# Seven block products for eight in 12 of the 16 d_ff tiles of the remaining tokens' second MLP product

## The chip, the cores and the metric

The kernel runs on one core of a Trainium2 chip. The metric is the device time of one execution in microseconds (us). Before the change the median of three runs is 258.58 us (258.47 to 258.95).

The engines are named as in the profile: PE (TensorE, matrix products), PEld (its weight loads), DVE (VectorE), ACT (ScalarE), POOL (GpSimd) and SP (SyncE, which here only issues DMAs).

## The reference

Polynomial-sketch attention, then an MLP with an exact GELU. B = 4 batches, H = 4 heads, S = 1088 tokens, D = 32; d_model = H x D = 128, d_ff = 2048; all in float32.

```python
def phi(x):                      # S1, S2: (8, 32)
    a = np.einsum('rd,bhsd->bhsr', S1, x)
    b = np.einsum('rd,bhsd->bhsr', S2, x)
    return np.einsum('bhsi,bhsj->bhsij', a, b).reshape(*x.shape[:-1], r * r)
q_p, k_p = (phi(q), phi(k))
kv = np.einsum('bhsf,bhsd->bhfd', k_p, v)
z = np.sum(k_p, axis=2)
num = np.einsum('bhsf,bhfd->bhsd', q_p, kv)
den = np.einsum('bhsf,bhf->bhs', q_p, z)[..., None] + 1e-06
x = (num / den).transpose(0, 2, 1, 3).reshape(B * S, H * D)
h = x @ w_in                     # (4352, 128) @ (128, 2048)
g = 0.5 * h * (1.0 + erf(h * inv_sqrt2))
out = g @ w_out                  # (4352, 2048) @ (2048, 128)
```

## The kernel before, in words

**Chunks and tiles.** The 4352 tokens are worked in nine chunks: eight of 512 tokens (n = 0 to 7, two for each batch, the first 1024 tokens of each), and a ninth (n = 8, called NMAIN in the code) of the 256 remaining tokens, 64 of each batch. d_ff is cut into 16 tiles of 128 (fi). A step is one pair (chunk, tile). `hidden` multiplies a tile of w_in by the chunk's transposed x (L739, 512 or 256 moving columns) into a bank of the pool `hps` (two banks), and ACT writes the GELU of it to SBUF (L746), as g in [d_ff, token] form. With `by_halves` the same product is issued as two matmuls of 64 stationary columns each, one for each half of the PE array, which run side by side.

**The second product of chunks 0 to 7.** In most tiles it is done with seven block products in place of eight (the Winograd form of Strassen's algorithm): tokens and channels are cut in halves and two d_ff tiles are the two halves of the inner dimension. POOL makes four sums of the activations (`token_sums`, L790 to L793, for four tiles at a time) and, once, four sums T1 to T4 of the halves of w_out (`channel_sums`, L777 to L780). The products (`two_products`, L825) have 64 stationary columns and run in pairs on the two halves of the PE array; `drain` and `combine` put the results together on DVE and ACT, and `store` transposes and stores them.

**The second product of the ninth chunk.** It is done whole, in [token, channel] form: `project` takes, for each tile, g of 128 tokens as the stationary operand and the tile of w_out (128 x 128) as the moving one, for each of the two token halves (L873; L876 is the same function's matmul for the first tiles of chunks 0 and 1). The two token halves accumulate in two banks, each taken with `work_bank` from the pool `wps`, which has two buffers. `store` copies the first half with DVE and issues its DMA from SP, and copies the second half with ACT and issues its DMA from ACT's queue (L882, L883).

**Order.** The order is written out by hand: for each step t the lists `slots`, `products`, `drains` and `done` say what is issued with it, and at the end every engine's instructions are bound to the order of the text. So PE, POOL, DVE and ACT each work through one fixed queue; an instruction that waits holds up all behind it on its engine. For the ninth chunk, step fi issues the hidden tile fi and then the second products put into that step: the first three tiles' in step 5, two tiles' in step 6, and then tile fi - 2 in step fi. After the last hidden tile, eight products are left, of tiles 12 to 15: three of token half 0, then half 1 of tile 12, the last of half 0, and the other three of half 1.

Of the kernel before, what the change touches and what calls it, by code (L numbers as in the profile page):

```python
# [8 lines left out]
FP = mybir.dt.float32  # L9
# [7 lines left out]
def kernel(  # L17
# [18 lines left out]
    pe, dve, act, pool, sp = nc.tensor, nc.vector, nc.scalar, nc.gpsimd, nc.sync  # L36
# [5 lines left out]
    NF = d_ff // 128  # L42
# [5 lines left out]
    CW = JC * 128  # L48
    G = 128 // 32
    NCH = J // JC  # L50
    C = D + 1
    LAG = 2
    NMAIN = B * NCH
    NB = 4

    USUAL = 8
    NCHUNK = NMAIN + 1
    assert B == 4 and d_model == 128 == H * D == JC * D == 2 * F and H == 4 and REM == 64 and NCH == 2

    big = ctx.enter_context(tc.tile_pool(name="big", bufs=1))  # L60
    att = ctx.enter_context(tc.tile_pool(name="att", bufs=2))
    mlp = ctx.enter_context(tc.tile_pool(name="mlp", bufs=2))
# [8 lines left out]
    def work_bank():  # L71
        return work_banks()[:, 0]
# [11 lines left out]
    by_act, by_dve, by_pool = act.copy, dve.tensor_copy, pool.tensor_copy  # L84
# [12 lines left out]
    w_out_sb = [big.tile([128, c1 - c0], FP, name=f"w_out{i}") for i, (c0, c1) in enumerate(pieces)]  # L97
# [96 lines left out]
    for i, (queue, s) in enumerate(((act, S1), (sp, S2))):  # L194
        s, e = words(s)
# [528 lines left out]
    g_of, o_of = {}, {}  # L724

    def w_tile(w, fi):
        i = max(i for i, (c0, c1) in enumerate(pieces) if c0 <= fi * 128)
        at = fi * 128 - CUTS[i]
        return w[i][:, at:at + 128]
# [3 lines left out]
    def hidden(n, fi, by_halves=False):  # L733
        W = width[n]
        ps = first_banks.pop((n, fi)) if (n, fi) in first_banks else hidden_bank()
        w = w_tile(w_in_sb, fi)
        for rows in (slice(0, 64), slice(64, 128)) if by_halves else (slice(0, 128),):
            if (n, fi) not in begun:
                pe.matmul(ps[rows, :W], lhsT=w[:, rows], rhs=xT[n][:, :W], start=True, stop=True)  # L739
        if n < NCH and fi < USUAL:  # L740
            g_of[n, fi] = mlp.tile([128, CW], FP, name="g", bufs=4)
        else:
            if fi % NB == 0:
                blocks[n, fi // NB] = block(FP)
            g_of[n, fi] = blocks[n, fi // NB][:, fi % NB]
        act.activation(out=g_of[n, fi][:, :W], in_=ps[:, :W], func=ACT.Gelu)  # L746
# [12 lines left out]
    blocks, sums, acc = {}, {}, {}  # L759
    T = {}  # L760
# [67 lines left out]
    drained = {}  # L828
# [26 lines left out]
    def combine(n):  # L855
# [6 lines left out]
            dve.tensor_add(out=N[:, 1], in0=N[:, 1], in1=usual[n])  # L862
        return N[:, 1]

    def project(n, fi, parts=range(B // 2), cols=slice(None)):
        first, final = fi == 0, fi == (USUAL if n < NCH else NF) - 1
        if first:
            o_of[n] = out_bank() if n < NMAIN else [work_bank() for i in range(B // 2)]
        g = g_of[n, fi]
        if n == NMAIN:  # L870

            for i in parts:
                pe.matmul(o_of[n][i][:, :128], lhsT=g[:, i * 128:(i + 1) * 128], rhs=w_tile(w_out_sb, fi),  # L873
                          start=first, stop=final)
            return
        pe.matmul(o_of[n][:, cols], lhsT=w_tile(w_out_sb, fi), rhs=g[:, cols], start=first, stop=final)  # L876

    def store(n):
        oT = mlp.tile([128, JC, d_model], FP, name="oT")
        if n == NMAIN:  # L880
            for i, copy, queue in ((0, by_dve, sp), (1, by_act, act)):
                copy(out=oT[:, i, :], in_=o_of[n][i][:, :128])  # L882
                queue.dma_start(out=out.rearrange("(two b s) d -> two b s d", two=2, s=S)[:, i, MAIN:S, :].rearrange("two s d -> s two d"),  # L883
                             in_=oT[:, i, :])
            return

        dve.transpose(out=oT.rearrange("p n d -> p (n d)"), in_=combine(n))
        row = n // NCH * S + n % NCH * CW
        if n < NCH:

            for c in range(d_model // 32):
                to = out[0:MAIN, c * 32:(c + 1) * 32].rearrange("(g t n j) d -> n j t g d", t=32, n=NCH, j=JC)[n]
                o = oT[c * 32:(c + 1) * 32].rearrange("p n (m d) -> p (n m) d", d=32)
                o = o.rearrange("p (g j) d -> j p g d" if n == 0 else "p (j g) d -> j p g d", j=JC)
                for j in range(JC):
                    sp.dma_start(out=to[j], in_=o[j])
            return
        to = out[row:row + CW].rearrange("(t n) d -> t n d", t=32)
        of = oT.rearrange("p n (m d) -> p (n m) d", d=32)
        for at in (slice(0, 16),) if n != NMAIN - 2 else (slice(0, 8), slice(8, 16)):  # L900
            for c in range(d_model // 32):
                sp.dma_start(out=to[:, at, c * 32:(c + 1) * 32], in_=of[c * 32:(c + 1) * 32, at])
# [46 lines left out]
    for c in range(NP):  # L949
        rows = slice(c * F, (c + 1) * F)  # L950
# [202 lines left out]
    for t, (n, fi) in enumerate(steps):  # L1153
        if n < NCH and fi < USUAL:
            products[t + LAG].append((project, n, fi))
            if fi == USUAL - 1:
                slots[t + LAG + 1 + 2 * n].append(lambda n=n: take_usual(n))
        elif n == NMAIN:
            at_ = max(t + LAG, (n * NF + 5) if fi < 3 else (n * NF + 6) if fi < 5 else 0)
            if fi < NF - 4:  # L1160
                products[at_].append((project, n, fi))
            if fi == NF - 1:

                products[at_] += [(project, n, NF - f, (i,)) for f, i in ((4, 0), (3, 0), (2, 0), (4, 1), (1, 0), (3, 1),
                                                                          (2, 1), (1, 1))]
                done[at_ + 1].append(n)
        elif fi % NB == NB - 1:
            b = fi // NB
            opens = b == first_block(n)
            late = int(n < NCH or n == NCH and opens)  # L1170
            for later, pairs in ((3, 3), (4, 2), (5, 2)) if opens else ((2, 2), (3, 2), (4, 1), (5, 2)):
                later += late
                for i in range(pairs):
                    products[t + later].append((two_products, n, b, len([p for q in products.values() for p in q
                                                                        if p[:3] == (two_products, n, b)])))
            if b == NF // NB - 1:
                drains[t + 6 + late].append(n)
                done[t + 12].append(n)

    for t in range(len(steps) + LAG):  # L1180
        if t < 4:

            hidden(0, t)
            if t == 0:
                expand_multiply(1, 0)
                w_out[0].fields()
                expand_copy(1, 1)
                expand_multiply(1, 1)
            if t == 1:
                w_out[0].low_words()  # L1190
                w_out[0].exponents()
                w_out[0].finish()
                w_out[1].fields()
            if t == 2:
                w_out[1].low_words()
            if t == 3:
                banks = work_banks()
                numerators_by_token(1, halves(banks), range(JC))
                w_out[1].mantissas(by_pool=True)
                w_out[1].exponents()  # L1200
                divide(1, halves(banks), 0)
                w_out[1].signs()
                w_out[1].product()
                project(0, 0)
                project(0, 1, cols=slice(0, 256))
                turn_half(1, 0, work_bank(), by_act)
                project(0, 1, cols=slice(256, 512))
                turn_half(1, 1, work_bank(), by_dve)
            continue
        if t == 4:  # L1210
            first_hidden(1, 0)
            for f, *a in products[t]:
                f(*a)
            first_hidden(1, 1)
        for n in drains[t]:
            drain(n)
        sooner = t == NMAIN * NF
        if sooner:
            for f, *a in products[t]:
                f(*a)  # L1220
        if t < len(steps):
            n, fi = steps[t]
            hidden(n, fi, by_halves=t >= 18 and (n < NMAIN or fi < 5))
        if t < len(steps) and steps[t][0] < NMAIN and steps[t][1] % NB == NB - 1:
            n, b = steps[t][0], steps[t][1] // NB
            if b >= first_block(n):
                token_sums(n, b)
        for f in slots[t]:
            f()
        for n in done[t]:  # L1230
            store(n)
        if t != 4 and not sooner:
            for f, *a in products[t]:
                f(*a)
# [41 lines left out]
```

## Time and profile before

| | |
|---|---|
| median of three runs | 258.58 us |
| the profiled execution's own time | 258.97 us |
| its span, first to last instruction | 257.2 us |
| PE busy | 253.0 us (98%) |
| POOL busy | 164.5 us (64%) |
| DVE busy | 151.6 us (59%) |
| ACT busy | 114.7 us (45%) |
| granted TensorE clock | 1.0 throughout |
| last POOL operation (chunk 7's sums) starts | 238.88 us |
| hidden tile 5 of the ninth chunk starts | 241.85 us |
| ACT's copy of the last output starts | 254.05 us |

How it is read: a PE line counts passes; a float32 matmul is two passes, and the two matmuls that run side by side on halves of the array start within 10 ns of each other. Shapes are written as array rows x stationary columns ("128\*64"), then the moving operand. The duration of one PE instruction contains its way through the array, so the rate is read from the distance between starts.

### The profile page before, as it was taken

To read this page: it belongs to the slowest core of one execution; us is meant where nothing else is said; L and a number is where in the kernel's file an instruction comes from. 1 tells how busy PE (TensorE), PEld (TensorE's weight loads), DVE (VectorE), ACT (ScalarE), POOL (GpSimd) and SP (SyncE) were. 2 spreads that over 40 slices of the span, in tenths; PEclk is the share of its full clock that TensorE was granted. 3 is DMA by queue.
4 is the path that set the end of the run, shared out by engine and by line. 5 is a ranking of instruction groups with operands and counts; after the bars stand their busy time and mean duration, and the time that the engine had idled before them with its cause. 6 is when DMAs were issued, how large, how long until landed. Compare 5 with 4: busy or idle time off the path is not lost.

```text
span 257.2 us, 5633 instructions
## 1 busy us (share of the span) xinstructions
PE 253.0 (98%) x2265; PEld 133.4 (52%) x2265; DVE 151.6 (59%) x314; ACT 114.7 (45%) x222; POOL 164.5 (64%) x175
## 2 busy tenths in 40 slices
PE   8999999999999999999999999999999999999995
PEld 4856444255444545454444455445544444445794
DVE  4896888969698987580278976399307000700330
ACT  3784767533535333533335332623444334433442
POOL 3414007799968787587758774787758777877300
PEclk9999999999999999999999999999999999999999
DMA  6699558710001101102000001000200200020020
GB/s 205 176 320 307 146 128 205 198 17 9 0 0 18 26 4 23 20 10 33 0 3 0 0 15 31 1 4 0 34 10 11 33 0 4 9 32 3 0 41 23
DMA packets 29082, 13.48 MB, mean 52 GB/s; under 512 B 21888, under 2 KB 27264, under 8 KB 29056
## 3 DMA queue, kind: packets, MB, share of 16 engines
q1 hardware_dynamic: 28624, 12.79, 20.2%
q8 instruction: 18, 0.29, 0.5%
q10 hardware_dynamic: 432, 0.33, 0.4%
q14 instruction: 8, 0.07, 0.1%
HBM read 10.88 MB, written 2.23 MB: 51 GB/s over the span
## 4 chain that ended last, share of the span: by engine, by line
PE 98%; ACT 0%; issue 0%
PE h_ps L739 45%; PE o_ps L825 33%; PE o_ps L876 5%; PE w_ps L873 3%; PE w_ps L455 1%; PE w_ps L603 1%; PE w_ps L658 1%; PE w_ps L908 1%; PE w_ps L569 1%; PE h_ps L755 1%; PE h_ps L347 1%; PE o_ps L444 1%; PE w_ps L994 1%; PE w_ps L684 0%; PE o_ps L396 0%; PE w_ps L485 0%
## 5 line engine op out<-in xcount | busy, mean ns | idle before, releaser
L739 PE MATMUL h_ps<-xT,w_in 128*64 128x512 f32 (+3 forms) x514 | 137.0, 576 | 0.0
L746 ACT ACTIVATE block<-h_ps 128x512 f32<-128x512 f32 (+1 forms) x128 | 73.0, 571 | 117.3 <-PE h_ps L739 115.3
L739 PEld LDWEIGHTS h_ps<-xT,w_in 128*64 128x64 f32 (+1 forms) x514 | 41.8, 142 | 30.6 <-issue 11.6
L825 PE MATMUL o_ps<-block,w_out 128*64 128x256 f32 x224 | 57.5, 379 | 0.0
L790 POOL TENSOR_TENSOR bits_low<-block 128x512 f32<-128x512 f32 x28 | 36.1, 1291 | 27.2 <-ACT block L746 27.2
L825 PEld LDWEIGHTS o_ps<-block,w_out 128*64 128x64 f32 x224 | 30.5, 137 | 38.0 <-issue 27.5
L791 POOL TENSOR_TENSOR bits_a<-block 128x512 f32<-128x512 f32 x28 | 35.8, 1277 | 11.7 <-ACT block L746 11.6
L840 DVE COPY sums<-o_ps 64x256 f32<-64x256 f32 x8 | 3.3, 416 | 60.6 <-PE o_ps L825 60.6
L792 POOL TENSOR_TENSOR bits_e<-bits_a,block 128x512 f32<-128x512 f32 x28 | 36.0, 1287 | 2.2
L793 POOL TENSOR_TENSOR bits_m<-block,bits_e 128x512 f32<-128x512 f32 x28 | 36.0, 1286 | 2.2
L825 PE MATMUL o_ps<-bits_a,small 128*64 128x256 f32 x112 | 28.8, 379 | 0.0
L825 PE MATMUL o_ps<-block,small 128*64 128x256 f32 x112 | 28.8, 379 | 0.0
L825 PE MATMUL o_ps<-bits_low,small 128*64 128x256 f32 x112 | 28.8, 379 | 0.0
L825 PE MATMUL o_ps<-bits_m,w_out 128*64 128x256 f32 x112 | 28.7, 379 | 0.0
L825 PEld LDWEIGHTS o_ps<-block,small 128*64 128x64 f32 x112 | 15.2, 137 | 17.9 <-issue 10.8
L825 PE MATMUL o_ps<-bits_e,small 128*64 128x256 f32 x112 | 17.1, 383 | 0.0
L876 PE MATMUL o_ps<-g,w_out 128*128 128x512 f32 (+1 forms) x34 | 16.5, 572 | 0.0
L825 PEld LDWEIGHTS o_ps<-bits_m,w_out 128*64 128x64 f32 x112 | 15.3, 137 | 0.0
L825 PEld LDWEIGHTS o_ps<-bits_a,small 128*64 128x64 f32 x112 | 15.2, 137 | 0.0
L825 PEld LDWEIGHTS o_ps<-bits_low,small 128*64 128x64 f32 x112 | 15.2, 137 | 0.0
L615 DVE STREAM_TRANSPOSE w_ps<-w_ps 128x512 f32<-128x512 f32 (+1 forms) x7 | 4.8, 688 | 17.1 <-ACT xT L669 12.7
L825 PEld LDWEIGHTS o_ps<-bits_e,small 128*64 128x64 f32 x112 | 7.7, 137 | 10.6 <-issue 8.8
(201 smaller groups left out, 302.6 us busy)
## 6 DMA issues: line engine op xcount, KB each, us to landing
block<-in_moe_w_in_dram SPq DMA_DIRECT2D x3, 512.0 KB, 10.3
block<-in_moe_w_out_dram SPq DMA_DIRECT2D x3, 512.0 KB, 10.4
k<-in_k_dram SPq DMA_DIRECT2D x12, 128.0 KB, 2.7
v<-in_v_dram SPq DMA_DIRECT2D x12, 128.0 KB, 3.2
q<-in_q_dram SPq DMA_DIRECT2D x24, 64.0 KB, 2.5
out_dram<-oT SPq DMA_DIRECT2D x21, 64.0 KB, 2.2
q_first<-in_q_dram SPq DMA_DIRECT2D x2, 256.0 KB, 4.2
v<-in_v_dram SPq DMA_DIRECT2D x2, 256.0 KB, 4.8
```

Source lines behind the costliest of these rows:

```text
L347: pe.transpose(ps[:, i * 128:(i + 1) * 128], in_=s, identity=ident)
L615: dve.transpose(out=tok, in_=ps[:, :, :H2])
L739: pe.matmul(ps[rows, :W], lhsT=w[:, rows], rhs=xT[n][:, :W], start=True, stop=True)
L746: act.activation(out=g_of[n, fi][:, :W], in_=ps[:, :W], func=ACT.Gelu)
L790: pool.tensor_sub(out=s[3], in0=a11, in1=a21)
L791: pool.tensor_add(out=s[1], in0=a21, in1=a22)
L792: pool.tensor_sub(out=s[2], in0=s[1], in1=a11)
L793: pool.tensor_sub(out=s[4], in0=a12, in1=s[2])
L825: pe.matmul(acc[n][bank][half * 64:(half + 1) * 64, col:col + HW], lhsT=fixed, rhs=moving, start=opens and e == 0 and name in "4715", stop ...
L840: dve.tensor_copy(out=N[lo, 0, one], in_=a0[lo, one])
L873: pe.matmul(o_of[n][i][:, :128], lhsT=g[:, i * 128:(i + 1) * 128], rhs=w_tile(w_out_sb, fi), start=first, stop=final)
L876: pe.matmul(o_of[n][:, cols], lhsT=w_tile(w_out_sb, fi), rhs=g[:, cols], start=first, stop=final)
```

## The change

The constant BLOCKED = 12 is added. For tiles 0 to 11 of the ninth chunk, `project` is replaced by seven block products for each pair of tiles (k = 0 to 5), with the roles of the operands as in `project`: activations (128 tokens) are stationary, w_out or one of its sums (64 channels) is moving. A block product is issued as two matmuls of 64 tokens each, on the two halves of the PE array. All seven of the sums' results lie beside each other in one bank, `acc`, 64 columns each.

- `sums_rem` (new, POOL): four sums of 128 x 128 for each pair of tiles, issued with the odd tile's step, behind chunk 7's sums.
- `product_rem` (new, PE): the 6 x 7 products, spread over steps 5 to 15, three or four in each, in the order "4127563" for each k.
- `combine_rem` (new, DVE): seven operations that turn the seven accumulated results into the four blocks of the output, in SBUF, issued with step 15.
- `project` handles tiles 12 to 15 only, after the last hidden tile, in the order of before. Its two banks are now taken when tile 12 comes, after `acc`.
- `store`: for both halves DVE adds the result of `combine_rem` to that of `project`; the ACT copy is gone. The DMAs are issued from the same queues as before.
- `hidden` of the ninth chunk is issued in halves for tiles 0 to 11 (before: 0 to 4).

```diff
+    BLOCKED = 12
...
+    ORDER_REM = "4127563"
+    COLS_REM = {name: slice(i * 64, (i + 1) * 64) for i, name in enumerate("1267543")}
+
+    def sums_rem(k):
+        g = [g_of[NMAIN, 2 * k + i][:, :256].rearrange("p (half x) -> p half x", half=2) for i in range(2)]
+        (a11, a21), (a12, a22) = ([a[:, h] for h in range(2)] for a in g)
+        s = mlp.tile([128, CW], FP, name="g", bufs=4).rearrange("p (j x) -> p j x", j=4)
+        pool.tensor_sub(out=s[:, 2], in0=a11, in1=a21)
+        pool.tensor_add(out=s[:, 0], in0=a21, in1=a22)
+        pool.tensor_sub(out=s[:, 1], in0=s[:, 0], in1=a11)
+        pool.tensor_sub(out=s[:, 3], in0=a12, in1=s[:, 1])
+        sums[NMAIN, k] = s
+
+    def product_rem(k, name):
+        if k == 0 and name == ORDER_REM[0]:
+            acc[NMAIN] = work_bank()
+        s = sums[NMAIN, k]
+        if name in "12":
+            fi = 2 * k + int(name) - 1
+            tokens, fixed = g_of[NMAIN, fi][:, 0:128], w_tile(w_out_sb, fi)[:, 0:64]
+        elif name == "3":
+            tokens, fixed = s[:, 3], w_tile(w_out_sb, 2 * k + 1)[:, 64:128]
+        elif name == "4":
+            tokens, fixed = g_of[NMAIN, 2 * k + 1][:, 128:256], T[4][:, k]
+        else:
+            j = "567".index(name)
+            tokens, fixed = s[:, j], T[j + 1][:, k]
+        for i in range(2):
+            rows = slice(i * 64, (i + 1) * 64)
+            pe.matmul(acc[NMAIN][rows, COLS_REM[name]], lhsT=tokens[:, rows], rhs=fixed,
+                      start=k == 0 and name == ORDER_REM[0], stop=k == BLOCKED // 2 - 1, skip_group_check=True)
+
+    def combine_rem():
+        p = acc[NMAIN][:, :7 * 64].rearrange("p (k d) -> p k d", d=64)
+        to, u = (att.tile([128, 2, CW], FP, name="sums")[:, 0] for i in range(2))
+        to = to[:, :256].rearrange("p (half c d) -> p half c d", half=2, c=2)
+        u = u[:, :320].rearrange("p (k d) -> p k d", k=5)
+        two = [128, 2, 64]
+        dve.tensor_copy(out=u[:, 0], in_=p[:, 0])
+        dve.tensor_add(out=u[:, 1:3], in0=p[:, 1:3], in1=u[:, 0:1].broadcast_to(two))
+        dve.tensor_add(out=u[:, 3:5], in0=p[:, 3:5], in1=u[:, 2:3].broadcast_to(two))
+        dve.tensor_copy(out=to[:, 0, 0], in_=u[:, 1])
+        dve.tensor_add(out=to[:, 0, 1], in0=p[:, 6], in1=u[:, 4])
+        dve.tensor_add(out=to[:, 1, 1], in0=p[:, 4], in1=u[:, 3])
+        dve.tensor_add(out=to[:, 1, 0], in0=p[:, 5], in1=u[:, 3])
+        drained[NMAIN] = to
+
     def project(n, fi, parts=range(B // 2), cols=slice(None)):
-        first, final = fi == 0, fi == (USUAL if n < NCH else NF) - 1
-        if first:
+        first, final = fi == (BLOCKED if n == NMAIN else 0), fi == (USUAL if n < NCH else NF) - 1
+        if first and n not in o_of:
             o_of[n] = out_bank() if n < NMAIN else [work_bank() for i in range(B // 2)]
...
-            for i, copy, queue in ((0, by_dve, sp), (1, by_act, act)):
-                copy(out=oT[:, i, :], in_=o_of[n][i][:, :128])
+            for i, queue in ((0, sp), (1, act)):
+                dve.tensor_add(out=oT[:, i, :], in0=o_of[n][i][:, :128], in1=drained[n][:, i].rearrange("p c d -> p (c d)"))
...
-            at_ = max(t + LAG, (n * NF + 5) if fi < 3 else (n * NF + 6) if fi < 5 else 0)
-            if fi < NF - 4:
-                products[at_].append((project, n, fi))
+            if fi % 2 and fi < BLOCKED:
+                slots[t].append(lambda k=fi // 2: sums_rem(k))
+            at_ = t + LAG
             if fi == NF - 1:
+                names = [(k, name) for k in range(BLOCKED // 2) for name in ORDER_REM]
+                steps_rem = NF - 5
+                for i, (k, name) in enumerate(names):
+                    products[n * NF + 5 + i * steps_rem // len(names)].append((product_rem, k, name))
+                products[n * NF + 4 + steps_rem].append((combine_rem,))
...
-            hidden(n, fi, by_halves=t >= 18 and (n < NMAIN or fi < 5))
+            hidden(n, fi, by_halves=t >= 18 and (n < NMAIN or fi < BLOCKED))
```

## The prediction

> **What bounds the kernel now.** I read the page first (busy time, then the chain of work that ended last), next the chain over the last 17 us, then the timeline of TensorE, GpSimd and VectorE at the places that price the new operations.
>
> ```profile
> PE 253.0 (98%) x2265; PEld 133.4 (52%) x2265; DVE 151.6 (59%) x314; ACT 114.7 (45%) x222; POOL 164.5 (64%) x175
> PE 98%; ACT 0%; issue 0%
> ```
>
> TensorE is the chain: 98% of the span. Any TensorE microsecond in the tail moves the end, and all edits lie in the tail, after the last product of chunk 7:
>
> ```profile
> 241.06 0.86 PE o_ps L825 x8
> 241.92 0.63 PE h_ps L739 x2
> 242.55 1.34 PE w_ps L873 x12
> ...
> 250.92 0.45 PE w_ps L873 x4
> 251.36 0.86 PE h_ps L739 x4
> 252.23 1.80 PE w_ps L873 x16
> ...
> 254.05 0.27 ACT oT L882
> ```
>
> The columns are start, duration, work, instructions; a fp32 matmul is two of these (two passes). One d_ff tile of the second product (L873, four passes) takes 0.446 (0.1115 a pass, 1.80 for 16), one hidden tile (L739, two passes) 0.43. TensorE never pauses until ScalarE's copy at 254.05. Three stretches of TensorE's timeline price what is new:
>
> ```profile
> 17.72 0.59 PE L739 MATMUL h_ps<-xT,w_in 128*128 128x512 f32 x1
> 18.24 1.16 PE L684 MATMUL w_ps<-kz_apart,q_pT 128*64 128x66 f32 x32
> 19.33 0.70 PE L876 MATMUL o_ps<-g,w_out 128*128 128x512 f32 x1
> ...
> 54.79 1.08 PE L455 MATMUL w_ps<-k_p,v 128*32 128x64 f32 x64
> 55.68 0.29 PE L455 MATMUL w_ps<-k_p_rem,v_rem_aug 128*32 128x64 f32 x8
> ...
> 241.54 0.38 PE L825 MATMUL o_ps<-bits_m,w_out 128*64 128x256 f32 x1
> 241.85 0.70 PE L739 MATMUL h_ps<-xT,w_in 128*128 128x256 f32 x2
> 242.39 0.39 PE L873 MATMUL w_ps<-w_out,block 128*128 128x128 f32 x2
> ```
>
> "128\*64" is a matmul on half of the array's columns (two run abreast), "128\*128" on all. Watch where the width changes.
>
> **Part 1, the products: -0.67.** Removed: 12 tiles at 0.446 = 5.35. Added: 6 x 7 block products, each a pair of half-width matmuls with 64 moving columns, two passes. L455 has 64 moving columns, four abreast: 64 records, 16 steps, 55.68 - 54.79 = 0.89, so 0.0557 a step and 0.1115 a pair. L684 is exactly this shape but for 66 columns: 16 steps in 1.09, less about 0.15 lost at its ends (part 2), is 0.0587, 0.117 a pair. 42 x 0.1115 = 4.68 (L684's price unscaled: 4.93, then only -0.42). I take 4.68, since the L455 step has the same number of columns. In halves the hidden tiles 5 to 11 cost what they cost whole: 0.43.
>
> **Part 2, changes of width: +1.38.** Before, the tail changes width once: the step from 241.54 to 241.85 is 0.31 where this shape steps by 0.215 (0.10 lost), and the two passes of the first full-width tile take 242.39 - 241.85 = 0.54 where 0.43 is usual (0.11 more): 0.20 a change from half to full. From full to half: 18.24 - 17.72 = 0.52 where a 512-column pass takes 0.43, 0.09 lost, and about 0.05 for the first load: 0.145. After the change, the products are half-width and the hidden tiles 12 to 15 still full-width (by_halves ends at BLOCKED), so the order is pairs, full, pairs, full, ... full: into full width at tiles 12, 13, 14, 15 and at the last projections (5), back four times. 4 more x 0.20 + 4 x 0.145 = 1.38. The least these rows allow is 8 x 0.145 = 1.16, the most 8 x 0.20 = 1.60.
>
> **Part 3, the wait at the end: +0.95.** The pool of w_ps tiles has two buffers. Before, the two output banks of the remaining tokens used both. Now acc takes one at tile 5, and o_of asks for two more at tile 12: the second is acc's own buffer. So the first product of token half 1, fourth of the last eight, must wait until combine_rem has read acc. Clock: from 241.75, 11 hidden tiles 4.74, pairs 4.68, changes up to the last pair 1.38: the last pair is streamed at 252.55, its result out at 252.71 (a pass begun at 252.49 lasts 0.22). The three products ahead are done at 252.55 + 0.20 + 0.67 = 253.42. VectorE's chain of seven:
>
> ```profile
> 156.53 0.23 DVE L621 COPY q_ac<-w_ps 128x64 f32<-128x64 f32 x1
> 156.79 0.23 DVE L622 TENSOR_TENSOR q_ac<-w_ps,q_ac 128x64 f32<-128x64 f32 x1
> ...
> 169.14 0.29 DVE L622 TENSOR_TENSOR q_ac<-w_ps,q_ac 128x128 f32<-128x128 f32 x1
> 169.47 0.29 DVE L624 TENSOR_REDUCE w_ps<-q_ac 128x32 f32<-128x128 f32 x1
> ```
>
> A dependent 64-wide step takes 0.26, a 128-wide one 0.33; independent ones start about 0.08 before the last has ended (the drain's L842 to L844: 0.33 for an operation of 0.41). So 0.26 + 0.33 + 0.21 + 3 x 0.145 + 0.225 = 1.45. With 0.05 for each handover (ScalarE's copy starts about 0.04 after the last pass ends), TensorE gets the bank at 252.76 + 1.45 + 0.05 = 254.26: 0.84 idle, plus 0.11 for a weight load that nothing covers. The least is 0.6 (a chain of 1.1, two of the small operations wholly beside others), the most 1.5 (all seven dependent: 5 x 0.26 + 2 x 0.33 = 1.96).
>
> **Part 4, GpSimd's sums: 0.** Four 128x128 operations a pair of tiles, in the queue behind chunk 7's last sum:
>
> ```profile
> 66.82 0.45 POOL L777 TENSOR_TENSOR small<-w_out 128x128 f32<-128x128 f32 x1
> 67.24 0.45 POOL L778 TENSOR_TENSOR small<-w_out 128x128 f32<-128x128 f32 x1
> 67.65 0.45 POOL L779 TENSOR_TENSOR small<-w_out,small 128x128 f32<-128x128 f32 x1
> 68.18 0.47 POOL L780 TENSOR_TENSOR small<-w_out,small 128x128 f32<-128x128 f32 x1
> ...
> 238.88 1.28 POOL L793 TENSOR_TENSOR bits_m<-block,bits_e 128x512 f32<-128x512 f32 x1
> ```
>
> 0.42 independent, 0.53 dependent: 0.42 + 0.53 + 0.53 + 0.42 = 1.90 a pair of tiles, from 238.88 + 1.24 = 240.12. TensorE needs a pair every 1.57 at first, so its lead shrinks to 0.4 at the "6" of the fourth pair (ready 247.2, wanted 247.7); then the width changes slow TensorE and the last sum is ready at 251.5, wanted at 252.4. So it hides, by little; without that slack a late sum stops TensorE, and with it the hidden tile queued behind and its GELU. Slowed sums (the first L777 to L780, beside VectorE's rounding, took 0.64 to 0.91) are a rival below.
>
> **Part 5, the store: +0.02.** VectorE's add (0.29, L622) replaces ScalarE's copy (0.27) at the end; the DMA of half 1 is still issued by ScalarE, half 0's by SP. The add also inherits four semaphore waits on earlier stores (50 ns each at L882, 245.9 to 246.2): they run while VectorE waits for half 0, 0.7 after the chain; uncovered they would cost 0.4.
>
> **Sum.** -0.67 + 1.38 + 0.95 + 0.02 = +1.68. The profiled execution took 258.97 (span 257.2); its sum is 260.65. It stands 0.39 above the median of the three runs, so against the median 258.58 I forecast 260.3.
>
> **Rivals.**
> *The end is not set by TensorE.* After 254.05 there are 3.1 us to the span's end; if more than 1.68 of them were something that runs whenever the store comes, the time would stay at 258.6. Against: DMA still moves 41 GB/s in that stretch, and the chain's last link is the copy that feeds the store.
> *Changes of width are free*, the loss at 241.85 being the wait for ScalarE of that load. Then TensorE meets GpSimd: the last "3" waits for its sum at 251.59, the chain ends at 253.3, and the sum is +0.75: 259.3. Against: at 243.73 a full-width hidden tile that also waits for ScalarE follows full-width products without loss (242.39 + 12 x 0.1115 = 243.73). The Trainium skill, "TensorEngine Tiling (Array Packing)", Key Properties, says that changing the tiling mode, not just the tile, drains TensorE; by that rule too this rival falls, but the page gives no price.
> *No wait for the bank* (part 3 gone): the eight products run through, the two adds follow the chain at 254.2 and the last product at 254.7: +0.7, 259.3. Against: two buffers, three tiles.
> *Weight loads are not hidden under 64 columns*: 84 steps, each with the 0.05 that a half-width load shows after a change: +4.2, 264.5. Against: L684, whose loads are of this size, steps at 0.0587. The Trainium skill, "TensorE: Matmul & The Clock Gate", The mechanism, says that a load overlaps a running matmul only if its row group differs, which it never does here; with that page's columns/1.2 ns (section LDWEIGHTS) a load would be 53 ns, and by this estimate the sum +6.1. Row L684 disagrees, so the chance is small.
> *GpSimd is late*: at the slow pace (2.9 us a pair of tiles, 41.46 to 44.38) the last sum would come at 257.5, +5; a tail that is slowed only while VectorE drains chunk 7 (to 247) costs up to 1. Against: GpSimd's operation at 220.75 kept its 1.27 beside that drain.
>
> **Chances.** Forecast 0.84 (the bounds of parts 1 to 3 give +1.1 to +2.6, so 259.7 to 261.2 is its own range); free changes 0.03; no bank wait 0.04; GpSimd late 0.05; exposed loads 0.01; end not set by TensorE 0.03. The range reaches down over the two cases at 259.3 and up over a mild GpSimd delay: 259.2 to 261.2. About 0.2% (0.5 us) is what a measurement here can tell from no change. No single case ends faster: 0.02 for what I have not seen, taken from the forecast; same 0.03; slower 0.95.
>
> **What would show it.** Right: steps of 0.31 and first tiles of 0.54 at hidden tiles 12 to 15; a TensorE gap of about 0.8 in the last eight products, released by VectorE; 42 pairs at 0.11; GpSimd operations of 0.45 ending by 251.6; span near 258.9. Wrong: no steps at the changes, TensorE idle on GpSimd, or no gap at the end.

## The result and the profile after

The changed kernel takes 260.75 us (median of six; 258.76 before, on the same chips): ratio 1.0073, 95% interval 1.0058 to 1.0089, so 1.5 to 2.3 us slower. The forecast was 260.3, slower.

The execution profiled with this result, one of six, ran at a granted TensorE clock of 0.947 and took 270.17 us (the ratio leaves it out), so the lines below are from a second profile of the same kernel (experiment 1, clock 0.999, 261.03 us, span 259.2). Its last product of chunk 7 starts 0.08 us later after the span's start than in the profile before; times of the two are compared with that taken off.

In the changed kernel L740 is `hidden`, L895 `product_rem`, L904 to L910 `combine_rem`, L921 the matmul of `project` and L930 the add of `store`; on GpSimd L794 is chunk 7's last sum and L873 to L876 are `sums_rem`.

The chain of the tail, start and duration:

```profile
242.00 0.43 PE h_ps L740 x4
242.44 0.47 PE w_ps L895 x16
242.90 0.43 PE h_ps L740 x4
...
247.71 0.47 PE w_ps L895 x16
248.17 0.63 PE h_ps L740 x2
248.80 0.61 PE w_ps L895 x16
249.42 0.63 PE h_ps L740 x2
...
252.53 0.52 PE w_ps L895 x12
253.06 0.02 issue
253.08 0.24 DVE sums L904
...
254.62 1.37 PE w_ps L921 x10
255.99 0.02 issue
256.01 0.29 DVE oT L930
```

Three things are read from it. Four pairs (16 passes) take 0.47 where nothing changes width: 0.117 a pair. From tile 12 on (248.17) a hidden tile takes 0.63 in place of 0.43, and the same four pairs 0.61 in place of 0.47: 0.20 into full width, 0.14 back. And at 253.06 the chain leaves TensorE for VectorE. TensorE's own timeline at that place shows the gap and who ended it:

```profile
252.75 0.29 PE L895 MATMUL w_ps<-w_out,g 128*64 128x64 f32 x4
252.96 0.94 PE L921 MATMUL w_ps<-w_out,block 128*128 128x128 f32 x6
254.62 1.35 PE L921 MATMUL w_ps<-w_out,block 128*128 128x128 f32 x10 [0.73 <-DVE sums L910]
```

Of the last eight products three (six passes) run; the fourth starts at 254.62, released by the last operation of `combine_rem`. Run through, it would have started at 252.96 + 0.10 (the first load after the change of width, part 2) + 6 x 0.1115 = 253.73: 0.89 lost, and 0.07 more for a weight load in the open (1.35 for ten passes, of which nine steps of 0.1115 and the last pass's 0.275 explain 1.28).

GpSimd's queue in the same execution:

```profile
238.95 1.28 POOL L794 TENSOR_TENSOR bits_m<-block,bits_e 128x512 f32<-128x512 f32 x1
240.18 0.46 POOL L873 TENSOR_TENSOR g<-block 128x128 f32<-128x128 f32 x1
...
245.47 0.52 POOL L876 TENSOR_TENSOR g<-block,g 128x128 f32<-128x128 f32 x1
245.95 0.64 POOL L873 TENSOR_TENSOR g<-block 128x128 f32<-128x128 f32 x1
...
251.40 0.46 POOL L876 TENSOR_TENSOR g<-block,g 128x128 f32<-128x128 f32 x1
```

The last sum is ready at 251.86, and the last pair, which needs it, starts at 252.75: hidden by 0.9.

### The profile page after: what moved, and what is told of

Read it like the earlier page. It is cut to its first block, busy times and chain, and to the rows that moved or that the text cites. A ratio compares the mean times of both kernels' runs of the same rounds, so it can differ in the third digit from the quotient of the medians.

```text
span 268.3 us, 5935 instructions
## 1 busy us (share of the span) xinstructions
PE 263.5 (98%) x2399; PEld 134.1 (50%) x2399; DVE 152.1 (57%) x322; ACT 114.7 (43%) x221; POOL 175.5 (65%) x199
## 4 chain that ended last, share of the span: by engine, by line
PE 98%; DVE 1%; issue 0%; DVEq 0%
PE h_ps L740 45%; PE o_ps L826 33%; PE o_ps L924 5%; PE w_ps L895 2%; PE w_ps L456 1%; PE w_ps L604 1%; PE w_ps L659 1%; PE w_ps L956 1%; PE w_ps L570 1%; PE h_ps L756 1%; PE o_ps L445 1%; PE w_ps L1042 1%; PE h_ps L348 1%; PE w_ps L921 1%; PE w_ps L685 0%; PE o_ps L397 0%
## 5 line engine op out<-in xcount | busy, mean ns | idle before, releaser
L740 PE MATMUL h_ps<-xT,w_in 128*64 128x512 f32 (+3 forms) x528 | 143.0, 593 | 0.0
L826 PE MATMUL o_ps<-block,w_out 128*64 128x256 f32 x224 | 59.7, 391 | 0.0
L740 PEld LDWEIGHTS h_ps<-xT,w_in 128*64 128x64 f32 (+1 forms) x528 | 41.7, 143 | 32.6 <-issue 12.5
L826 PEld LDWEIGHTS o_ps<-block,w_out 128*64 128x64 f32 x224 | 31.1, 140 | 40.5 <-issue 29.2
L794 POOL TENSOR_TENSOR bits_m<-block,bits_e 128x512 f32<-128x512 f32 x28 | 35.8, 1280 | 2.2
L826 PE MATMUL o_ps<-bits_low,small 128*64 128x256 f32 x112 | 29.9, 391 | 0.0
L826 PE MATMUL o_ps<-block,small 128*64 128x256 f32 x112 | 29.9, 391 | 0.0
L826 PE MATMUL o_ps<-bits_a,small 128*64 128x256 f32 x112 | 29.9, 391 | 0.0
L826 PE MATMUL o_ps<-bits_m,w_out 128*64 128x256 f32 x112 | 29.8, 391 | 0.0
L924 PE MATMUL o_ps<-g,w_out 128*128 128x512 f32 (+1 forms) x34 | 17.2, 595 | 0.0
```

The costliest lines, as they stand in the source:

```text
L794: pool.tensor_sub(out=s[4], in0=a12, in1=s[2])
L826: pe.matmul(acc[n][bank][half * 64:(half + 1) * 64, col:col + HW], lhsT=fixed, rhs=moving, start=opens and e == 0 and name in "4715", stop ...
```

## The experiments

The theory is the prediction's: changes of array width and the wait for the bank. The rivals are its rivals: changes that are free, a wait that does not delay the end, a late GpSimd. Each kernel ran beside the kernel before on the same chip.

**1. The changed kernel again.** No edit.

> The changed kernel once more, for a trace at the full granted clock. Theory (width changes cost 0.20 into full and 0.145 into half, and TensorE waits for the bank): 1.7 us more than before; TensorE gap of 0.8 us before the fourth of the last eight products; the last GpSimd sum ends by 251.6 us, about 0.9 before it is wanted. Rival (GpSimd is late): TensorE gaps that GpSimd releases.

Measured: 260.87 against 258.71, ratio 1.0081 (1.0067 to 1.0095): 2.2 us, 0.5 more than the sum. The gap is there and VectorE releases it; the last GpSimd sum is early enough. So the mechanisms stand and a size is off: the pairs, which are about half of the 0.5 (below).

**2. Hidden tiles 12 to 15 in halves: eight of nine width changes gone.**

```diff
-            hidden(n, fi, by_halves=t >= 18 and (n < NMAIN or fi < BLOCKED))
+            hidden(n, fi, by_halves=t >= 18)
```

> Changed kernel, with hidden tiles 12 to 15 of the ninth chunk in halves too: eight of the nine width changes are gone, the wait for the bank stays. Theory: TensorE is 1.38 faster up to the last pair, until it meets GpSimd, whose last sum is ready at 251.54: a new gap of about 0.4 there, and the time is 0.9 us below the changed kernel, 0.75 above before. Rival (width changes are free): the time of the changed kernel, 0. Rival (GpSimd does not bind even then): 1.38 below the changed kernel.

Measured: 259.86, 1.0 below experiment 1 (0.8 by the tails of the two traces, 13.90 for 14.68); ratio to before 1.0046 (1.0033 to 1.0059). Free changes would have left the time. The gain is less than the changes' own 1.4, as expected, because TensorE now meets GpSimd. Its timeline:

```profile
248.87 0.52 PE L895 MATMUL w_ps<-small,g 128*64 128x64 f32 x12
249.55 0.34 PE L895 MATMUL w_ps<-w_out,g 128*64 128x64 f32 x4 [0.17 <-POOL g L876]
249.72 0.60 PE L740 MATMUL h_ps<-xT,w_in 128*64 128x256 f32 x4
```

Three pairs from 248.87 are streamed by 249.22; the "3" of the fifth pair of tiles starts at 249.55 only, when its sum has come. The width changes had hidden GpSimd.

**3. The output banks apart from acc.**

```diff
-            o_of[n] = out_bank() if n < NMAIN else [work_bank() for i in range(B // 2)]
+            o_of[n] = out_bank() if n < NMAIN else halves(work_banks())
```

> Changed kernel, but the two output banks of the last four tiles are the two banks of one w_ps tile, so that acc keeps the other buffer to itself. Theory: the gap of 0.84 and the uncovered weight load of 0.11 go; VectorE's chain then ends about when the last product does, and the time is 1.0 us below the changed kernel, 0.7 above before. Rival (the wait is not what delays the end): within 0.3 of the changed kernel.

Measured: 260.22, 0.65 below experiment 1; ratio 1.0048 (1.0035 to 1.0062). The gap is gone, but less than 1.0 was gained:

```profile
252.84 2.05 PE L921 MATMUL w_ps<-w_out,block 128*128 128x128 f32 x16
...
254.14 0.21 DVE L910 TENSOR_TENSOR sums<-w_ps,sums 128x64 f32<-128x64 f32 x1
254.93 0.49 DVE L930 TENSOR_TENSOR oT<-w_ps,sums 128x128 f32<-128x128 f32 x2 [0.57 <-PE w_ps L921]
```

The sixteen passes run without a pause. The chain ends at 254.35, yet both adds start after the last product, at 254.93, in a row: the add of half 0 now waits for the last writer of a tile that holds both halves. That costs about 0.2 (the last add ends at 255.42; one add alone would have ended at 255.22) and was no part of the expectation. In experiment 5, where the halves are two tiles, the first add starts when the chain ends.

**4. Width changes added to the kernel before, and nothing else.**

```diff
-            hidden(n, fi, by_halves=t >= 18 and (n < NMAIN or fi < 5))
+            hidden(n, fi, by_halves=t >= 18 and (n < NMAIN or fi < 5 or fi in (7, 9, 11, 13)))
```

> The kernel before, with hidden tiles 7, 9, 11 and 13 of the ninth chunk in halves between full-width products: eight width changes are added and nothing else. Theory: 4 x 0.345 = 1.38 us slower than before (between 1.16 and 1.60). Rival (the loss at a change is the wait of that load for ScalarE): 0.

Measured: 260.38, ratio 1.0059 (1.0047 to 1.0072): 1.2 to 1.9 us. Counted from the last product of chunk 7 (241.49 here, 241.54 before) to the end of ScalarE's copy, the tail is 14.16 against 12.77: 1.39. The timeline at one of the four places:

```profile
246.65 0.61 PE L873 MATMUL w_ps<-w_out,block 128*128 128x128 f32 x4
247.19 0.65 PE L739 MATMUL h_ps<-xT,w_in 128*64 128x256 f32 x4
247.77 0.60 PE L873 MATMUL w_ps<-w_out,block 128*128 128x128 f32 x3
```

From 246.65 to 247.19 is 0.54 where four passes take 0.446, and from 247.19 to 247.77 is 0.58 where a hidden tile takes 0.43. The work is the same; only its width alternates. This decides the question of what changes of width cost: 1.39 / 4 = 0.35 for a change and back.

**5. No width change and no wait for the bank.** Hidden tiles as in 2; the second output bank from the pool of chunk 7's outputs; the last eight products in halves.

```diff
-            o_of[n] = out_bank() if n < NMAIN else [work_bank() for i in range(B // 2)]
+            o_of[n] = out_bank() if n < NMAIN else [work_bank(), out_bank()]
...
             for i in parts:
-                pe.matmul(o_of[n][i][:, :128], lhsT=g[:, i * 128:(i + 1) * 128], rhs=w_tile(w_out_sb, fi),
-                          start=first, stop=final)
+                for rows in (slice(0, 64), slice(64, 128)):
+                    pe.matmul(o_of[n][i][rows, :128], lhsT=g[:, i * 128:(i + 1) * 128][:, rows], rhs=w_tile(w_out_sb, fi),
+                              start=first, stop=final)
```

> Changed kernel without any width change (hidden tiles 12 to 15 and the last eight products in halves too) and without the wait for the bank (the second output bank comes from the pool of chunk 7's outputs, free by then). Theory: TensorE then meets GpSimd, whose last sum comes at 251.5, and runs its last eight products from 251.6 to 253.4; 0.4 us below before, 2.5 below the changed kernel. Rival (something else in the change costs time): still above before.

Measured: 258.64, ratio 0.9992 (0.9976 to 1.0009): 2.2 below experiment 1, but no faster than before that can be told. Nothing else in the change costs time that can be told. The interval, from 0.6 faster to 0.2 slower, holds both no gain and the 0.4 expected; by the traces the tail is 12.75 against 12.77, so the gain is not seen there. The end of its chain:

```profile
248.86 0.07 issue
248.93 0.47 POOL g L876
249.40 0.04 issue
249.44 0.34 PE w_ps L895 x4
...
251.34 0.34 PE w_ps L895 x4
251.67 0.66 PE w_ps L922 x12
```

The chain runs through GpSimd up to 249.40, and at 251.34 the last pair again waits for its sum. The last product of chunk 7 starts at 241.02 in this execution, 0.53 earlier than in the profile before, so on that clock the last pair starts at 251.87 and the last eight products (251.50 in TensorE's timeline) at 252.03, not at 251.6. Of this about 0.25 is GpSimd, later than its rows of 0.42 and 0.53 gave, and 0.16 is the last pair itself, which the expectation left out. Where GpSimd loses its 0.25 is seen in experiment 1: 0.52 and 0.64 for the operations at 245.47 and 245.95, beside two adds of chunk 7's results on VectorE that read SBUF alone. In experiment 1:

```profile
245.10 0.57 DVE L860 TENSOR_TENSOR sums<-sums 64x256 f32<-64x256 f32 x1
245.68 0.59 DVE L861 TENSOR_TENSOR sums<-sums 64x256 f32<-64x256 f32 x1
```

The same two adds in the profile before:

```profile
245.02 0.42 DVE L859 TENSOR_TENSOR sums<-sums 64x256 f32<-64x256 f32 x1
245.45 0.42 DVE L860 TENSOR_TENSOR sums<-sums 64x256 f32<-64x256 f32 x1
```

The adds take 0.42 each where GpSimd is done, and 0.57 and 0.59 in experiment 1, where GpSimd's 0.46 becomes 0.52 and 0.64: both engines are slower while they meet. The Trainium skill, "GPSIMD Engine Reference", section 8, Key points, says that GpSimd shares its SBUF interfaces with VectorE and names VectorE instructions with two SBUF inputs as a cause of contention; the trace agrees, with these durations.

**6. Ten tiles in place of twelve.** As 5, but the block products of five pairs of tiles over steps 5 to 14, and tiles 10 and 11 as whole products in steps 14 and 15.

```diff
-    BLOCKED = 12
+    BLOCKED = 10
...
-                steps_rem = NF - 5
+                steps_rem = NF - 6
...
                 products[n * NF + 4 + steps_rem].append((combine_rem,))
+                for f in range(BLOCKED, NF - 4):
+                    products[n * NF + f + 4].append((project, n, f))
```

> As e5, but seven products for eight in 10 tiles instead of 12; tiles 10 and 11 go through whole products in the last two steps, the pairs over ten steps. Theory: GpSimd's last sum (249.6) is early enough; TensorE does 35 pairs at 0.117 (4.10) and 6 tiles at 0.446 (2.68) in place of 16 at 0.446 (7.14), and loses no 0.20: 0.36 + 0.20, so 0.55 us below before. Rival (seven products for eight gain nothing at these sizes): not below the kernel before with everything in halves (e7).

Measured: 258.06, ratio 0.9972 (0.9961 to 0.9983): 0.4 to 1.0 us faster than before, and the fastest of all kernels here. The last sum no longer delays, and VectorE's chain lies wholly under TensorE's last work:

```profile
249.10 0.46 POOL L876 TENSOR_TENSOR g<-block,g 128x128 f32<-128x128 f32 x1
249.44 0.40 PE L895 MATMUL w_ps<-small,g 128*64 128x64 f32 x8
249.67 0.29 PE L895 MATMUL w_ps<-w_out,g 128*64 128x64 f32 x4
...
251.18 0.21 DVE L910 TENSOR_TENSOR sums<-w_ps,sums 128x64 f32<-128x64 f32 x1
...
252.18 0.83 PE L922 MATMUL o_ps<-w_out,block 128*64 128x128 f32 x12
...
253.06 0.29 DVE L931 TENSOR_TENSOR oT<-o_ps,sums 128x128 f32<-128x128 f32 x1 [0.36 <-PE o_ps L922]
```

**7. The kernel before, all in halves.** The `project` edit of 5 and the `hidden` edit of 2 in the kernel before.

> The kernel before, with all hidden tiles and all second products of the ninth chunk in halves: its one width change is gone. Theory: 0.20 us below before. Rival (free changes): 0.

Measured: 258.51, ratio 0.9987 (0.9979 to 0.9996): 0.1 to 0.5 us faster. Putting everything in halves, which removes the one change of width, pays by itself. From the last product of chunk 7 to the end of the last copy its tail is 12.43, against 12.77 before and 12.17 in experiment 6. So of the 0.60 that experiment 6 gains in the tail, 0.34 is there with everything in halves (0.20 was expected; the last section has the rest) and only 0.26 is left for seven products in place of eight.

**8. Each block product in two, of 32 moving columns.**

```diff
-        for i in range(2):
-            rows = slice(i * 64, (i + 1) * 64)
-            pe.matmul(acc[NMAIN][rows, COLS_REM[name]], lhsT=tokens[:, rows], rhs=fixed,
-                      start=k == 0 and name == ORDER_REM[0], stop=k == BLOCKED // 2 - 1, skip_group_check=True)
+        for c, i in ((c, i) for c in range(2) for i in range(2)):
+            rows, at_ = slice(i * 64, (i + 1) * 64), COLS_REM[name].start + c * 32
+            pe.matmul(acc[NMAIN][rows, at_:at_ + 32], lhsT=tokens[:, rows], rhs=fixed[:, c * 32:(c + 1) * 32],
+                      start=k == 0 and name == ORDER_REM[0] and c == 0, stop=k == BLOCKED // 2 - 1, skip_group_check=True)
```

> Changed kernel, each block product issued as two with 32 moving columns in place of one with 64: the same columns in twice as many weight loads. If the load of 64 stationary columns sets the step (0.0585, whatever the moving columns), each of the 42 pairs costs 0.117 more: 4.9 us above the changed kernel. If the moving columns set it (64 x 2 at the rate of the 128-column passes): at most 0.3 above.

Measured: 265.43, ratio 1.0254 (1.0237 to 1.0272), 4.6 above experiment 1, near the 4.9 expected if the load decides. Half the moving columns do not make a step shorter. Alone, this would fit a fixed price for each pass as well; two rows of the profile before, both with 33 moving columns, decide against that:

```profile
9.17 0.61 PE L444 MATMUL o_ps<-sums,k_p 128*64 128x33 f32 x16
...
9.71 0.46 PE L444 MATMUL o_ps<-sums,k_p 128*32 128x33 f32 x32
```

Each row holds eight passes one behind the other, two matmuls abreast in the first and four in the second. With the last pass taken off (0.22 and 0.20) a step is 0.39 / 7 = 0.056 with 64 stationary columns, and 0.26 / 7 = 0.037 with 32. So the load of 64 stationary columns sets the step, and no fixed price does. The profile before shows the price with 64 moving columns too:

```profile
5.97 0.69 PE L396 MATMUL o_ps<-S,kT 128*64 128x64 f32 x16 [0.24 <-ACT kT L349]
6.49 0.64 PE L396 MATMUL h_ps<-S,kT 128*64 128x64 f32 x16
```

Eight steps in 0.52, less the 0.05 of the first load: 0.0587, the price of L684 with its 66 columns. L455, whose 0.0557 I took, has only 32 stationary columns.

## Why the prediction was right, and what was off

The forecast's direction and both mechanisms (changes of width, the wait for the bank) held, and the time lies in the range. By its own steps, with the tail of experiment 1 measured against that of before (14.68 against 12.77 from the last product of chunk 7 to the end of the last output operation, +1.9; the sum said +1.68):

| part | predicted | measured | from |
|---|---|---|---|
| 1 products | -0.67 | -0.44 | 42 pairs at 0.117 = 4.91 for 5.35 |
| 2 changes of width | +1.38 | +1.4 | 4 x 0.35; experiment 4: 1.39 in the tail |
| 3 wait for the bank | +0.95 | +0.96 | 0.89 of gap, 0.07 for the load |
| 4 GpSimd's sums | 0 | 0 | last sum 0.9 before it is wanted |
| 5 store | +0.02 | +0.02 | 0.29 for 0.27 |

The measured parts add to 1.94.

*The term that was mis-sized is part 1.* "I take 4.68, since the L455 step has the same number of columns" matched the wrong number: a step's price follows the stationary columns here, and the row with the same stationary columns, L684, had been given as the other bound (-0.42). Experiment 8 and the rows of L444 beside it show that the load decides. The Trainium skill, "TensorE: Matmul & The Clock Gate", section LDWEIGHTS, gives a load as columns/1.2 ns, by this estimate 53 ns for 64; the steps of 0.0585 agree with it as a floor under the step, while the rival that adds the load to the stream (0.0557 + 0.05) is refuted by the 0.117 of a pair.

*Part 2* was right to a few hundredths, and experiments 2, 4 and 7 take away, add and take away changes of width with the expected sign. The rival of free changes falls. That TensorE would then meet GpSimd was in that rival's sum (0.75 above before; experiment 2: 0.9 to 1.5).

*Part 3.* The chain took 1.39 (253.08 to 254.47) for 1.45 predicted, and the handover back to TensorE 0.15 where 0.05 was put; the weight load in the open cost 0.07 for 0.11. The gap and the load come to 0.96 for 0.95, then, because errors of up to 0.10 cancel: the wait was right, the closeness is luck. The rival without this wait falls. With the wait removed by another bank, experiment 3 gained 0.65, not 1.0. By the tails of the traces (14.68 and 13.92) it gained 0.76, and the shared tile explains the 0.2 that is missing from the 0.96; the remaining 0.1 of the medians is less than the scatter of its runs (259.72 to 260.31).

*Part 4.* GpSimd was hidden, as predicted, but its sums come 0.25 late because they meet VectorE's work on chunk 7. The 0.9 left at the last sum, as forecast, is luck: TensorE, with its dearer pairs, also wants that sum about 0.25 later. Where the forecast saw the least room, at the "6" of the fourth pair of tiles, 0.35 was left for 0.4 (ready at 247.54, started at 247.89). The lateness costs nothing in the changed kernel, and it shows in experiments 2 and 5. So a small part of the rival "GpSimd is late" is real. The row given against it, GpSimd's 1.27 at 220.75, was read on one engine only; beside it VectorE's add took 0.82, not 0.42:

```profile
221.47 0.82 DVE L859 TENSOR_TENSOR sums<-sums 64x256 f32<-64x256 f32 x1
```

*Part 5 and the end.* From the end of the last output operation to the end of the span it is 2.87 us in the profile before and in experiment 1. So the rival "the end is not set by TensorE" falls: what follows that operation moves with it.

What stays open: the first comparison and experiment 1 give 1.99 and 2.16 by medians where the trace accounts for 1.9; the intervals cover it.

## What to carry to other kernels

Count the changes of array width before counting products: a switch to half-width matmuls and back costs TensorE 0.35 us here, as much as three of the block products it was to serve, so keep everything around them at one width. Price a short matmul by its stationary columns as well as its moving ones. And when a new accumulator comes from a pool, count the buffers that live at the end: the third tile of a pool of two waits for whoever reads the first.

## What the runs showed of the hardware that was not expected

With two 64-column loads side by side and 128 rows, a pass steps by 0.0585 us with 32, 33, 64 or 66 moving columns; seven products for eight are then worth 0.892 - 0.819 = 0.07 us for a pair of d_ff tiles, not 0.11. And halves are slightly cheaper than the whole array at 128 moving columns. In experiment 7:

```profile
245.12 0.61 PE L874 MATMUL w_ps<-w_out,block 128*64 128x128 f32 x8
245.56 0.60 PE L739 MATMUL h_ps<-xT,w_in 128*64 128x256 f32 x4
245.99 0.61 PE L874 MATMUL w_ps<-w_out,block 128*64 128x128 f32 x8
```

The chain before:

```profile
250.04 0.44 PE w_ps L873 x4
250.48 0.43 PE h_ps L739 x2
```

A second product and a hidden tile take 0.867 in halves (245.12 to 245.99) and 0.88 whole (250.04 to 250.92, where the next L873 follows). Over the tail's eleven hidden tiles and sixteen second products this fits the 0.14 by which experiment 7 gained more than the 0.20 of its one change. Against second products in halves (0.437 each, 245.12 to 245.56), seven for eight are worth only 0.874 - 0.819 = 0.055 us for a pair of tiles: 0.27 for five pairs, near the 0.26 of experiment 6.
